# Two-layer feed-forward behind a delta-rule attention: weight splits by DMA, an early output factor, and the first substitution on another engine

## The chip, the cores and the metric

The kernel runs on one core of one Trainium2 chip. The time is the device time of one execution in microseconds; of several executions the median counts. An execution that was profiled leaves a trace: its span runs from the first to the last instruction. PE is the matrix engine, DVE, ACT and POOL are the vector, scalar and general engines, SP issues the transfers (DMA).

## The reference

A linear attention with the delta rule, then two feed-forward blocks on the heads put side by side (4 x 768 tokens, 8 heads of 48, so 384 features; hidden size 2048):

```python
k_n = k / (np.linalg.norm(k, axis=-1, keepdims=True) + 1e-06)
for t in range(S):
    y[:, :, t] = np.einsum('bhd,bhde->bhe', q[:, :, t], state)
    v_old = np.einsum('bhde,bhd->bhe', state, kt)
    state = state + bt[:, :, :, None] * np.einsum('bhd,bhe->bhde', kt, vt - v_old)
x = y.transpose(0, 2, 1, 3).reshape(B * S, H * D)
h = x @ w_in;  x = np.maximum(0.01 * h, h) @ w_out        # first block
h = x @ w2_in; x = (h - np.tanh(h)) @ w2_out              # second block
```

## The kernel before

**Data.** Every float32 operand of a matmul is split into two f16 parts, a high one and the rest (low), and a product is three matmuls: high x high, high x low, low x high. The four weight matrices arrive as 64-bit words; three integer instructions on DVE (`w_f32`: one tensor_scalar and two scalar_tensor_tensor) make float32 of them, in the place that the f16 parts will take. A weight is scaled by a power of two (`sw`), which needs its squared norm first. `Weights.splits` (L415) then goes over the 16 chunks of 384 columns of a matrix: ACT writes a scaled float32 copy `wst`, ACT makes the high half from it, and `tt` takes the difference on DVE or POOL. `wst` is a buffer of the ring "sx", of four buffers, which the layers' activations, `xhi`, `kn` and the output `osb` share.

**Work.** The 768 tokens are 12 stretches of 64 (n = 0 to 11), in 6 pairs u. For each pair the keys are normalized (`key_scale`, L547, a Newton iteration on DVE in small instructions), Gram matrices are made, and a triangular matrix of 32 x 32 for each of 32 blocks is inverted by forward substitution (`inverses`, L669): for column j a product and a sum, each over (31 - j) x j elements of a partition, 30 columns, 60 dependent instructions. Then come merges, states and outputs, which give x for n. The first block is layer (n, 0), the second layer (n, 1): eight steps `h_part` (18 matmuls of 256 columns), activation, split, and `o_part`. Order: (0,0), (1,0), (0,1), (1,1), then the next pair. `out_scale` (L1021) computes the factor of the output, three instructions on one column, at the end of a second layer, before ACT and DVE copy half of the output each from PSUM into `osb`.

**Order.** The program is written out by a planner that keeps a clock for each engine and a cost for each instruction. All side work (keys, inverses, weights "w", splits "s0" to "s3" and so on) consists of generators; each yields the time from which it wants to go on, and the one with the smallest time plus its bias (`d_i`, `d_w`, ...) goes next. The engines run their instructions in the order so written, and SP its transfers. The biases and some counts are read from START until all weights are converted ("w2"), from STEADY afterwards. `rows` is the number of columns of blocks solved on POOL; the rest is solved on DVE:

```python
for j in range(1, rows - 1):
    solve(pool, j, j + 1, rows)          # yields every third column
...
while rows < HB and jd < HB - 1:         # HB = 32
    for jd in range(jd, min(jd + 3, HB - 1)):
        solve(dve, jd, max(jd + 1, rows), HB)
    yield plan.t["dve"] - tune("look_inv")
```

With `rows` 32 all is on POOL. Since every instruction is issued through the planner, all have line 160 in the profile; they are told apart by engine and tile (X and Gd: the substitution; wi, wo: weights; wst: the scaled copy).

Of the kernel before, what the change touches and what calls it, by code (L numbers as in the profile page):

```python
# [7 lines left out]
F32 = mybir.dt.float32  # L8
F16 = mybir.dt.float16
BF16 = mybir.dt.bfloat16  # L10
I32 = mybir.dt.int32
ACTF = mybir.ActivationFunctionType
ALU = mybir.AluOpType
# [3 lines left out]

KS = 64.0
POW2 = 0x7F800000
START = {'cp': 1.0, 'lag': 4.0, 'look_pool': 3, 'look_inv': 0, 'lead_k': 1, 'lead_p': 7.5, 'd_v': 1, 'd_xa': 0, 'd_xb': 1, 'k_m': 2, 'd_s0': 1.0, 'd_s1': 1.0, 'd_s2': -1, 'd_s3': 0.5, 'bias_i': 3.5, 'bias': 1.5, 'rep': 4, 'every': 3, 'd_k0': 3, 'd_o': 0.5, 'd_s': 0.0, 'd_p': 0, 'd_m': 0, 'd_i': 0, 'd_g0': -2, 'd_q': 4.4, 'd_g': 0.5, 'd_k': 1, 'd_w': 0, 'rows': 32}  # L20
STEADY = {'cp': 5.5, 'lag': 4.0, 'look_pool': 3, 'look_inv': 2.5, 'lead_k': 1, 'lead_p': 7.5, 'd_v': 1, 'd_xa': -1, 'd_xb': 1, 'k_m': 2, 'd_s0': 1.0, 'd_s1': 1.0, 'd_s2': -1, 'd_s3': 0.5, 'bias_i': 3, 'bias': 1, 'rep': 6, 'every': 2, 'd_k0': 3, 'd_o': 0.5, 'd_s': 0.0, 'd_p': 0, 'd_m': 0, 'd_i': 0, 'd_g0': 0, 'd_q': 3.4, 'd_g': 0.0, 'd_k': 0, 'd_w': 0, 'rows': 32}


# [168 lines left out]
def kernel(  # L192
# [23 lines left out]
    DM = KT * 128  # L216
# [27 lines left out]
    def mm(o, lhsT, rhs, start=True, stop=True):  # L244
        pe.matmul(out=o, lhsT=lhsT, rhs=rhs, start=start, stop=stop)

    def copy(o, i, scale=1.0):
        act.activation(out=o, in_=i, func=ACTF.Copy, scale=scale)
# [4 lines left out]
    def tt(o, a, b, op, lead=2.0):  # L253

        f = {e: plan.finish(e, "tensor_tensor", [a, b], [o]) for e in ("dve", "pool")}
        (dve if f["dve"] + lead < f["pool"] else pool).tensor_tensor(out=o, in0=a, in1=b, op=op)
# [5 lines left out]
    def bias():  # L262
        return tune("bias_i" if "inverse" in done else "bias")
# [13 lines left out]
    def lo_of(o, i, scale, hi):  # L277
        dve.scalar_tensor_tensor(out=o, in0=i, scalar=scale, in1=hi, op0=ALU.mult, op1=ALU.subtract)
# [97 lines left out]
    class Weights:  # L376
# [36 lines left out]
            done.add((self.i, "s"))  # L413

        def splits(self):  # L415
            for f in range(NF):
                yield plan.t["act"]
                w = s_p.tile([128, DM], F32, tag="sx", name="wst")
                copy(w, self.f32[:, f], sw[:, self.i:self.i + 1])
                copy(self.dst[:, f, 0], w)  # L420
                tt(self.dst[:, f, 1], w, self.dst[:, f, 0], ALU.subtract, bias())
                done.add((self.i, f))

    def weights():
        wi = [words(w.rearrange("p f c n -> p (f c n)")) for w in WI2]
# [121 lines left out]
    def key_scale(a, y, t):  # L547

        dve.tensor_scalar(out=t, in0=a, scalar1=2.0 ** -100, scalar2=None, op0=ALU.max)
        dve.tensor_scalar(out=y.bitcast(I32), in0=t.bitcast(I32), scalar1=1, scalar2=POW2,  # L550
                          op0=ALU.logical_shift_right, op1=ALU.bitwise_and)
        dve.tensor_scalar(out=t, in0=y, scalar1=2.0 ** 64 / 0.85, scalar2=None, op0=ALU.mult)
        dve.reciprocal(out=y, in_=t)
        for it in range(5):
            if it in (1, 3):
                yield plan.t["dve"]
            dve.tensor_tensor(out=t, in0=y, in1=y, op=ALU.mult)
            dve.scalar_tensor_tensor(out=t, in0=t, scalar=-0.5, in1=a, op0=ALU.mult, op1=ALU.mult)
            dve.scalar_tensor_tensor(out=y, in0=t, scalar=1.5, in1=y, op0=ALU.add, op1=ALU.mult)
        dve.tensor_tensor(out=t, in0=a, in1=y, op=ALU.mult)  # L560
        dve.tensor_scalar(out=t, in0=t, scalar1=1e-6, scalar2=1.0 / KS, op0=ALU.add, op1=ALU.mult)
        dve.reciprocal(out=y, in_=t)
# [403 lines left out]
    def h_part(i, x, p, kap):  # L966

        ps = ps_h.tile([128, 2 * N], F32, tag="h", name="h_ps")
        order = [(t, a, b) for t in range(KT) for a, b in ((0, 0), (0, 1), (1, 0))]
        if p == 0:  # L970
            order = [(t, a, 0) for t in range(KT) for a in range(2)] + [(t, 0, 1) for t in range(KT)]
        for j in range(2):
            for n, (t, a, b) in enumerate(order):
                mm(ps[:, j * N:(j + 1) * N], WI[i][:, 2 * p + j, a, t], x[b][:, t], n == 0, n == 3 * KT - 1)
                if n % tune("every") == tune("every") - 1:
                    side.step()
        sx = s_p.tile([128, 2 * N], F32, tag="sx", name="sx")
        if i == 0:
            act.activation(out=sx, in_=ps, func=ACTF.Prelu, scale=C0, alpha=0.01)
        else:  # L980
            act.activation(out=sx, in_=ps, func=ACTF.Tanh, scale=kap[:, 0:1])
            dve.scalar_tensor_tensor(out=sx, in0=sx, scalar=kap[:, 1:2], in1=ps, op0=ALU.mult, op1=ALU.add)
        g = g_p.tile([128, 2, 2 * N], F16, tag="g", name="g")
        if i == 0:
            copy(g[:, 0], sx)
            tt(g[:, 1], sx, g[:, 0], ALU.subtract, bias())
        else:
            split(g[:, 0], g[:, 1], sx, C0)
        return g

    def o_part(i, po, g, p):

        for j in range(2):
            f = 2 * p + j
            first, last = f == 0, f == NF - 1
            gj = g[:, :, j * N:(j + 1) * N]
            for o in range(KT if i == 0 else 2):
                if i == 0 and o == 0 and first:
                    mm(po[0], maskp[:, 0:1].to_broadcast([128, 128]), maskp[:, 0:1].to_broadcast([128, 512]), True, False)
                for n, (a, b) in enumerate(((0, 0), (0, 1), (1, 0))):  # L1000
                    if i == 0:
                        mm(po[o // 2][:, o % 2 * N:o % 2 * N + N], WO[0][:, f, a, o * 128:(o + 1) * 128], gj[:, b],
                           o == 2 and first and n == 0, o > 0 and last and n == 2)
                    else:
                        mm(po[o][:, 0:DM], gj[:, b, o * 128:(o + 1) * 128], WO[1][:, f, a], first and n == 0,
                           last and n == 2)
                side.step()

# [12 lines left out]
    def out_scale(kap):  # L1021
        dve.tensor_scalar(out=kap[:, 2:3], in0=sw[:, 3:4], scalar1=C0, scalar2=None, op0=ALU.mult)
        dve.reciprocal(out=kap[:, 3:4], in_=kap[:, 2:3])
        dve.tensor_tensor(out=kap[:, 2:3], in0=kap[:, 3:4], in1=kap[:, 0:1], op=ALU.mult)
# [80 lines left out]
    def o_next():  # L1105
        n, i, p, g, kap, sx, po = pend.pop(0)
        if p == 0:
            po += [ps_o.tile([128, 512], F32, tag=f"o{o}", name=f"o{o}") for o in range(2)]
        need((2 * i + 1, 2 * p + 1))
        side.step(plan.at(g, WO[i][:, 2 * p], WO[i][:, 2 * p + 1]))  # L1110
        o_part(i, po, g, p)
        if p < NP - 1:
            return
        if i == 0:
            gen = to_xb(n, po, sx)
            e = side.add(gen, "xb")
            side.advance(e)
            return
        out_scale(kap)
        for o in range(2):  # L1120
            ob = s_p.tile([128, DM], F32, tag="sx", name="osb")
            if o % 2:
                dve.tensor_scalar(out=ob, in0=po[o][:, 0:DM], scalar1=kap[:, 2:3], scalar2=None, op0=ALU.mult)
            else:
                copy(ob, po[o][:, 0:DM], kap[:, 2:3])
            for h in range(2):
                r0 = (2 * o + h) * S + n * C
                sp.dma_start(out=out[r0:r0 + C], in_=ob[h * C:(h + 1) * C])

    def layer(n, i):  # L1130
        if i == 0:
            while ("n", n) not in done:
                if pend:
                    o_next()
                else:
                    side.force()
            x, sx = xa_t.pop(n)
            kap = None
        else:
            while ("m", n) not in done:  # L1140
                if pend:
                    o_next()
                else:
                    side.force()
            x, sx = xb_t.pop(n)
            need((2, "s"))
            kap = kappa(sx)
        po = []
        for p in range(NP):
            need((2 * i, 2 * p + 1))  # L1150
            side.step(max(at(x[0], WI[i][:, 2 * p]), ps_h.free("h")))
            g = h_part(i, x, p, kap)
            pend.append((n, i, p, g, kap, sx, po))
            if len(pend) > LAG:
                o_next()
        done.add(("ab"[i], n))
# [78 lines left out]
```

## Time and profile before

| | us |
|---|---|
| median of 3 runs | 1221.16 (1218.24 to 1222.01) |
| the profiled execution | 1222.18 |
| its span | 1220.3 |
| PE busy | 1013.1 (83%) |
| DVE busy | 736.5 (60%) |
| ACT busy | 634.0 (52%) |
| POOL busy | 509.1 (42%) |

The shares are means over a first part in which the weights are prepared and the first pair is computed, and a long second part with layers on the PE. The granted clock of the PE over the span was 0.97 of full speed.

### The profile page before, as it was taken

To read this page: it belongs to the slowest core of one execution; us is meant where nothing else is said; L and a number is where in the kernel's file an instruction comes from. 1 tells how busy PE (TensorE), PEld (TensorE's weight loads), DVE (VectorE), ACT (ScalarE), POOL (GpSimd) and SP (SyncE) were. 2 spreads that over 40 slices of the span, in tenths; PEclk is the share of its full clock that TensorE was granted. 3 is DMA by queue.
4 is the path that set the end of the run, shared out by engine and by line. 5 is a ranking of instruction groups with operands and counts; after the bars stand their busy time and mean duration, and the time that the engine had idled before them with its cause. 6 is when DMAs were issued, how large, how long until landed. Compare 5 with 4: busy or idle time off the path is not lost.

```text
span 1220.3 us, 36850 instructions
## 1 busy us (share of the span) xinstructions
PE 1013.1 (83%) x16216; PEld 831.8 (68%) x16216; DVE 736.5 (60%) x1592; ACT 634.0 (52%) x1409; POOL 509.1 (42%) x635
## 2 busy tenths in 40 slices
PE   0301658898798989989999888899999999999998
PEld 0201547686686878857787766678867888778875
DVE  7997896857567567777755665546753064420243
ACT  3555679695356655645567534435543364333332
POOL 4597446388214872483332682485110321012100
PEclk9999999899898989989999898999999999999999
DMA  9423133100001000000111000001000000000001
GB/s 363 154 84 113 55 106 96 37 24 1 16 23 39 24 22 17 26 23 24 39 32 37 24 1 16 10 8 33 25 10 14 14 12 2 11 17 1 1 1 27
DMA packets 21857, 48.17 MB, mean 39 GB/s; under 512 B 4288, under 2 KB 7360, under 8 KB 21696
## 3 DMA queue, kind: packets, MB, share of 16 engines
q1 hardware_dynamic: 21696, 45.82, 11.9%
q8 instruction: 126, 2.06, 0.7%
q14 instruction: 35, 0.29, 0.1%
HBM read 41.09 MB, written 4.72 MB: 38 GB/s over the span
## 4 chain that ended last, share of the span: by engine, by line
PE 51%; DVE 26%; ACT 11%; POOL 8%; issue 4%; DMA 0%; ACTq 0%; SPq 0%; DVEq 0%; POOLq 0%
PE o L160 21%; PE h_ps L160 19%; PE a_ps L160 11%; DVE n L160 4%; POOL X L160 3%; POOL Gd L160 3%; DVE x L160 2%; ACT g L160 2%; DVE wi L160 2%; DVE g L160 2%; DVE sx L160 2%; DVE wo L160 2%; ACT junk L160 1%; ACT sx L160 1%; DVE X L160 1%
## 5 line engine op out<-in xcount | busy, mean ns | idle before, releaser
L160 PE MATMUL h_ps<-x,wi 128*128 128x256 f16 x3456 | 427.9, 276 | 18.3 <-DVE x L160 12.3
L160 PEld LDWEIGHTS <-wi 128*128 128x128 f16 x3456 | 336.5, 99 | 77.6 <-issue 23.6
L160 PE MATMUL o<-wo,g 128*128 128x384 f16 x1152 | 214.9, 337 | 25.5 <-ACT osb L160 16.0
L160 POOL TENSOR_TENSOR g<-sx,g 128x512 f16<-128x512 f32 x78 | 93.1, 1194 | 311.6 <-ACT g L160 291.6
L160 PE MATMUL o<-g,wo 128*128 128x256 f16 x1728 | 210.6, 275 | 0.0
L160 PEld LDWEIGHTS <-wo 128*128 128x128 f16 x1728 | 167.4, 98 | 32.3 <-issue 10.5
L160 ACT ACTIVATE g<-sx 128x512 f16<-128x512 f32 x192 | 121.0, 630 | 120.2 <-DVE sx L160 117.2
L160 PEld LDWEIGHTS <-g 128*128 128x128 f16 x1152 | 113.7, 100 | 96.0 <-issue 36.0
L160 DVE SCALAR_TENSOR_TENSOR sx<-sx,kap,h_ps 128x512 f32<-128x512 f32 x96 | 71.2, 741 | 92.9 <-ACT sx L160 92.6
L160 POOL TENSOR_TENSOR Gd<-X 128x30 f32<-128x30 f32 (+9 forms) x180 | 110.8, 616 | 33.3 <-DVE X L160 19.5
L160 POOL TENSOR_TENSOR X<-X,Gd 128x30 f32<-128x30 f32 (+9 forms) x180 | 114.8, 638 | 14.1
L160 DVE SCALAR_TENSOR_TENSOR g<-sx,g 128x512 f16<-128x512 f32 x96 | 74.3, 774 | 67.4 <-ACT g L160 67.4
L160 ACT ACTIVATE sx<-h_ps,kap 128x512 f32<-128x512 f32 x96 | 65.4, 681 | 81.6 <-PE h_ps L160 71.3
L160 ACT ACTIVATE sx<-h_ps 128x512 f32<-128x512 f32 x96 | 56.5, 589 | 93.9 <-PE h_ps L160 87.6
L160 PEld LDWEIGHTS <-KTp 64*64 64x64 f16 x3360 | 66.2, 118 | 36.4 <-issue 34.4
L160 POOL TENSOR_TENSOR P<-P,maskp 128x1024 f16<-128x1024 f16 x24 | 52.6, 2196 | 61.4 <-DVE P L160 58.2
L160 PE MATMUL a_ps<-ab,ones 128*128 128x1 bf16 x124 | 11.7, 168 | 75.3 <-DVE ab L160 73.4
L160 PEld LDWEIGHTS <-KN 64*64 64x64 f16 x1824 | 37.5, 120 | 39.7 <-issue 35.7
L160 PE MATMUL a_ps<-Q,Sb 128*128 128x64 f16 x528 | 35.7, 199 | 13.2 <-DVE Sb L160 13.2
L160 PEld LDWEIGHTS <-ones 128*128 128x128 bf16 x124 | 7.8, 102 | 54.0 <-DVE ab L160 50.0
L160 PE MATMUL a_ps<-Q,KTp 64*64 64x64 f16 x1152 | 25.4, 201 | 23.1 <-ACT Q L160 20.2
L160 ACT ACTIVATE x<-a_ps,qs 32x128 f32<-32x128 f32 (+1 forms) x57 | 25.5, 447 | 31.4 <-PE a_ps L160 28.2
(161 smaller groups left out, 1533.1 us busy)
## 6 DMA issues: line engine op xcount, KB each, us to landing
wo<-in_w_in_dram SPq DMA_DIRECT2D x32, 384.0 KB, 6.1
qf<-in_q_dram SPq DMA_DIRECT2D x24, 256.0 KB, 2.6
wi<-in_w_out_dram SPq DMA_DIRECT2D x14, 384.0 KB, 7.8
kf<-in_k_dram SPq DMA_DIRECT2D x12, 384.0 KB, 4.1
vf<-in_v_dram SPq DMA_DIRECT2D x12, 384.0 KB, 4.1
out_dram<-osb SPq DMA_DIRECT2D x48, 96.0 KB, 2.2
wo<-in_w_out_dram SPq DMA_DIRECT2D x8, 384.0 KB, 3.8
stage<-in_w_out_dram SPq DMA_DIRECT2D x8, 384.0 KB, 3.8
```

The costliest lines, as they stand in the source:

```text
L160: return getattr(self.eng[eng], op)(*args, **kw)
```

## The change

- START gets `rows` 2: while the weights are not all converted, a substitution runs on DVE, in ten batches of three columns, and so do the three instructions behind it.
- `splits` goes over two chunks at once: ACT writes the scaled high half in f16 into a ring buffer, DVE makes the low half from the float32 source, the scale and that high half, into the first f16 place of the chunk, and a DMA on SP copies the high half into the second place. The matmuls read the two places in swapped order (`1 - a`).
- `key_scale` starts its Newton iteration from a better estimate and makes three rounds instead of five.
- `out_scale` moves from the end of a second layer to its start, behind `kappa`.

```diff
-START = {..., 'rows': 32}
+START = {..., 'rows': 2}
         def splits(self):
-            for f in range(NF):
+
+            s_ = sw[:, self.i:self.i + 1]
+            for f in range(0, NF, 2):
                 yield plan.t["act"]
-                w = s_p.tile([128, DM], F32, tag="sx", name="wst")
-                copy(w, self.f32[:, f], sw[:, self.i:self.i + 1])
-                copy(self.dst[:, f, 0], w)
-                tt(self.dst[:, f, 1], w, self.dst[:, f, 0], ALU.subtract, bias())
-                done.add((self.i, f))
+                w = s_p.tile([128, 2, DM], F16, tag="sx", name="wh")
+                copy(w, self.f32[:, f:f + 2], s_)
+                lo_of(self.dst[:, f:f + 2, 0], self.f32[:, f:f + 2], s_, w)
+                sp.dma_start(out=self.dst[:, f:f + 2, 1], in_=w)
+                done.update((self.i, f + i) for i in range(2))
     def key_scale(a, y, t):
         dve.tensor_scalar(out=t, in0=a, scalar1=2.0 ** -100, scalar2=None, op0=ALU.max)
-        dve.tensor_scalar(out=y.bitcast(I32), in0=t.bitcast(I32), scalar1=1, scalar2=POW2,
-                          op0=ALU.logical_shift_right, op1=ALU.bitwise_and)
-        dve.tensor_scalar(out=t, in0=y, scalar1=2.0 ** 64 / 0.85, scalar2=None, op0=ALU.mult)
-        dve.reciprocal(out=y, in_=t)
-        for it in range(5):
-            if it in (1, 3):
+        dve.tensor_scalar(out=t.bitcast(I32), in0=t.bitcast(I32), scalar1=1, scalar2=None,
+                          op0=ALU.logical_shift_right)
+        dve.tensor_scalar(out=y.bitcast(I32), in0=t.bitcast(I32), scalar1=-1.0, scalar2=float(0x5F375A00),
+                          op0=ALU.mult, op1=ALU.add)
+        for it in range(3):
+            if it == 1:
                 yield plan.t["dve"]
...
-                mm(ps[:, j * N:(j + 1) * N], WI[i][:, 2 * p + j, a, t], x[b][:, t], n == 0, n == 3 * KT - 1)
+                mm(ps[:, j * N:(j + 1) * N], WI[i][:, 2 * p + j, 1 - a, t], x[b][:, t], n == 0, n == 3 * KT - 1)
...
-        out_scale(kap)
         for o in range(2):
             ob = s_p.tile([128, DM], F32, tag="sx", name="osb")
...
             kap = kappa(sx)
+            out_scale(kap)
```

`o_part` gets the same `1 - a` in both of its matmuls.

## Rows read from the trace of the kernel before

**Rows 1.** Windows by stage: length, busy us (instructions) of PE, PEld, DVE, ACT, POOL.

```profile
48.00:107.20 59.20, 2.84 (x83) 2.58 (x84) 52.97 (x79) 30.23 (x74) 52.87 (x66) 1.00 0.35 118
107.20:181.70 74.50, 35.97 (x1138) 34.05 (x1138) 65.69 (x111) 52.56 (x120) 36.87 (x33) 1.00 0.31 101
181.70:381.40 199.70, 177.63 (x2910) 144.28 (x2910) 132.99 (x302) 130.91 (x320) 96.99 (x120) 0.94 0.12 34
381.40:820.00 438.60, 397.51 (x7144) 325.20 (x7145) 284.20 (x646) 233.82 (x574) 233.02 (x317) 0.95 0.08 22
```

**Rows 2.** The chain of waits, 0 to 320 us, its shares by line.

```profile
by line: POOL X L160 12.6%; POOL Gd L160 10.4%; DVE wi L160 8.5%; issue 7.2%; DVE wo L160 6.1%; DVE n L160 6.0%; DVE x L160 3.5%; PE a_ps L160 3.4%; DVE X L160 2.5%; ACT g L160 2.2%; DVE g L160 1.7%; ACT wo L160 1.6%; POOL wi L160 1.6%; ACT
```

**Rows 3.** POOL's timeline: start, duration, instruction [idle before]; substitution's first, product with beta.

```profile
50.00 0.85 POOL L160 TENSOR_TENSOR Gd<-X 128x30 f32<-128x30 f32 x1 [2.81 <-DVE X L160]
...
107.26 2.34 POOL L160 TENSOR_TENSOR X<-X,bt 128x1024 f32<-128x1024 f32 x1
```

**Rows 4.** PE's timeline: first matmuls of layers (0, 0) and (2, 0).

```profile
181.70 5.79 PE L160 MATMUL h_ps<-x,wi 128*128 128x256 f16 x27 [5.57 <-DVE x L160]
...
381.45 0.93 PE L160 MATMUL h_ps<-x,wi 128*128 128x256 f16 x5 [1.28 <-DVE x L160]
```

**Rows 5.** DVE's timeline, 17 to 27 us: single durations.

```profile
17.76 0.95 DVE L160 SCALAR_TENSOR_TENSOR wi<-wo,wi 128x768 int32<-128x768 int32 x1
...
24.58 0.18 DVE L160 TENSOR_TENSOR x<-x 128x32 f32<-128x32 f32 x1
24.80 0.42 DVE L160 SCALAR_TENSOR_TENSOR x<-x 128x32 f32<-128x32 f32 x2
...
26.75 0.56 DVE L160 TENSOR_TENSOR kn<-kf,x 128x384 f32<-128x384 f32 x1
```

**Rows 6.** Groups by form on DVE, 50 to 107.2 us: busy us, mean ns.

```profile
L160 DVE SCALAR_TENSOR_TENSOR wo<-wi,wo 128x768 int32<-128x768 int32 x14 | 17.6, 1254 | 0.4
L160 DVE TENSOR_TENSOR wi<-wst,wi 128x384 f16<-128x384 f32 x8 | 8.0, 1002 | 2.1 <-ACT wi L160 2.1
L160 DVE SCALAR_TENSOR_TENSOR wi<-wo,wi 128x768 int32<-128x768 int32 x7 | 7.4, 1063 | 0.2
L160 DVE TENSOR_SCALAR wo<-wi 128x768 int32<-128x768 int32 x7 | 6.1, 872 | 0.0
L160 DVE SCALAR_TENSOR_TENSOR wo<-x,wo 128x384 int32<-128x384 int32 x4 | 4.2, 1063 | 0.0
```

**Rows 7.** Windows of the splits (tile wst): length, DVE, ACT, POOL; sum from 48 us.

```profile
107.20:181.70 74.50, 0.54 (x1) 26.23 (x48) 27.13 (x25) 1.00 0.31 101
...
sum 252.00, DVE 13.69 ACT 70.98 POOL 51.13; mean DVE 4.56 ACT 23.66 POOL 17.04
```

**Rows 8.** Groups by form, 0 to 320 us: the split of x on ACT and DVE.

```profile
L160 ACT ACTIVATE xhi<-x,sxs 128x768 f16<-128x768 f32 x4 | 3.7, 924 | 0.2 <-DVE n L160 0.2
...
L160 DVE SCALAR_TENSOR_TENSOR x<-x,sxs,xhi 128x768 f16<-128x768 f32 x4 | 4.1, 1020 | 5.1 <-ACT xhi L160 5.1
```

**Rows 9.** Timelines: the last weight scale, a split between pair 1's solve steps.

```profile
229.28 0.16 DVE L160 RECIPROCAL sw<-p 128x1 f32<-128x1 f32 x1
...
264.39 0.91 POOL L160 TENSOR_TENSOR wo<-wst,wo 128x384 f16<-128x384 f32 x1
```

**Rows 10.** DMA issues, 100 to 300 us: count, KB each, median us to landing.

```profile
qf<-in_q_dram SPq DMA_DIRECT2D x5, 256.0 KB, 2.6
```

**Rows 11.** Timelines at the end of layer (0, 1).

```profile
325.41 0.58 ACT L160 ACTIVATE osb<-o,kap 128x384 f32<-128x384 f32 x1 [1.28 <-DVE kap L160]
325.43 0.62 DVE L160 TENSOR_SCALAR osb<-o,kap 128x384 f32<-128x384 f32 x1
...
326.05 0.65 PE L160 MATMUL o<-wo,g 128*128 128x384 f16 x3 [4.15 <-ACT osb L160]
```

**Rows 12.** Tile osb, whole span: its own waits, then who waited for it.

```profile
  DVE kap L160: 13.0, 7
...
  PE o L160: 19.6, 8
```

More of the change, by code (lines that the diff above doesn't have):

```diff
@@ L19 @@
 POW2 = 0x7F800000
-START = {'cp': 1.0, 'lag': 4.0, 'look_pool': 3, 'look_inv': 0, 'lead_k': 1, 'lead_p': 7.5, 'd_v': 1, 'd_xa': 0, 'd_xb': 1, 'k_m': 2, 'd_s0': 1.0, 'd_s1': 1.0, 'd_s2': -1, 'd_s3': 0.5, 'bias_i': 3.5, 'bias': 1.5, 'rep': 4, 'every': 3, 'd_k0': 3, 'd_o': 0.5, 'd_s': 0.0, 'd_p': 0, 'd_m': 0, 'd_i': 0, 'd_g0': -2, 'd_q': 4.4, 'd_g': 0.5, 'd_k': 1, 'd_w': 0, 'rows': 32}
+START = {'cp': 1.0, 'lag': 4.0, 'look_pool': 3, 'look_inv': 0, 'lead_k': 1, 'lead_p': 7.5, 'd_v': 1, 'd_xa': 0, 'd_xb': 1, 'k_m': 2, 'd_s0': 1.0, 'd_s1': 1.0, 'd_s2': -1, 'd_s3': 0.5, 'bias_i': 3.5, 'bias': 1.5, 'rep': 4, 'every': 3, 'd_k0': 3, 'd_o': 0.5, 'd_s': 0.0, 'd_p': 0, 'd_m': 0, 'd_i': 0, 'd_g0': -2, 'd_q': 4.4, 'd_g': 0.5, 'd_k': 1, 'd_w': 0, 'rows': 2}
 STEADY = {'cp': 5.5, 'lag': 4.0, 'look_pool': 3, 'look_inv': 2.5, 'lead_k': 1, 'lead_p': 7.5, 'd_v': 1, 'd_xa': -1, 'd_xb': 1, 'k_m': 2, 'd_s0': 1.0, 'd_s1': 1.0, 'd_s2': -1, 'd_s3': 0.5, 'bias_i': 3, 'bias': 1, 'rep': 6, 'every': 2, 'd_k0': 3, 'd_o': 0.5, 'd_s': 0.0, 'd_p': 0, 'd_m': 0, 'd_i': 0, 'd_g0': 0, 'd_q': 3.4, 'd_g': 0.0, 'd_k': 0, 'd_w': 0, 'rows': 32}
@@ L1001, in o_part @@
                     if i == 0:
-                        mm(po[o // 2][:, o % 2 * N:o % 2 * N + N], WO[0][:, f, a, o * 128:(o + 1) * 128], gj[:, b],
+                        mm(po[o // 2][:, o % 2 * N:o % 2 * N + N], WO[0][:, f, 1 - a, o * 128:(o + 1) * 128], gj[:, b],
                            o == 2 and first and n == 0, o > 0 and last and n == 2)
                     else:
-                        mm(po[o][:, 0:DM], gj[:, b, o * 128:(o + 1) * 128], WO[1][:, f, a], first and n == 0,
+                        mm(po[o][:, 0:DM], gj[:, b, o * 128:(o + 1) * 128], WO[1][:, f, 1 - a], first and n == 0,
                            last and n == 2)
```

## The prediction

> **What bounds the kernel now.** I read the windows by stage first. In 48 to 107 us the PE is busy 2.8 of 59.2 us while DVE (53.0) and POOL (52.9) are full; in 107 to 181.7 the PE has half of the stretch and DVE 65.7 of 74.5; in 181.7 to 381.4 the PE is busy 178 of 200, then 398 of 439 [rows 1]. So the first 181.7 us are a prologue in which the PE starves, and behind it the PE is the bound with 22 and 41 us of idle time in those two. The chain of waits over the first 320 us says what the prologue is made of: POOL X and Gd (the forward substitution) on top, 23%, then DVE's weight words [rows 2]. On POOL's timeline the substitution of pair 0 runs from 50.0 to the product with beta, which ends at 107.26 + 2.34 = 109.6 [rows 3]. The first matmul of layer (0, 0) waits for x at 181.70, and that of pair 1 at 381.45, again for x with 1.28 us of idle PE [rows 4]: after each start a pair has 200 us of PE work, so an earlier first start is kept only if pair 1's x comes earlier too.
>
> **The substitution on DVE.** POOL loses 60 instructions, DVE gains 60 on the same shapes: twice the sum of j(31 - j), 9,920 elements per partition. DVE's price early in the run: 0.18 us for 32 elements, a dependent one starts 0.22 us after it, and 0.56 us for 384 elements, so 1.08 ns an element [rows 5]. That is 60 x 0.22 + (9,920 - 1,920) x 1.08 ns = 13.2 + 8.6 = 21.8 us. The upper bound is what company costs: the weights' tensor_tensor of 384 took 1.00 instead of 0.56 while POOL was busy [rows 5, 6], so 39 us. I take 21.8, since the work that kept POOL busy in this stretch is just what leaves it.
>
> Here one rule of the Trainium skill bears (SBUF — State Buffer, Who interferes with whom): a DVE instruction with two SBUF inputs and a POOL instruction that reads SBUF exclude each other, and the later one blocks. The rows agree that such DVE instructions stretch beside POOL [rows 5, 6]. By the rule the solve would take the low end as long as POOL is empty, and the same sum comes out.
>
> The DVE is shared, so what lies between the solve's ten batches decides. In 48 to 107 us the weight words took 25 scalar_tensor_tensor (17.6 + 7.4 + 4.2 us) and, by the code, 13 tensor_scalar (7 of them 6.1 us, so about 10.4), the splits 8.0 us; the rest of 53.0 is 5.4 [rows 1, 6]. A solve batch and the weights both ask again at the time DVE comes free, with the same bias 0, so I expect them to alternate: 11 weight instructions at 0.95 [rows 5], 10.5 us. W1_in's 8 new splits add 8.2 (price below). The end: 50.0 + 21.8 + 10.5 + 8.2 + 5.4 + 1.3 for the product with beta = 97.2 instead of 109.6, 12.4 us earlier. With none of the weights between it is 86.7 (22.9 earlier), with all 38 it is 122.8 (13.2 later); the break-even is 24.
>
> **The splits.** Before, 64 chunks cost ACT two activations each, 71 us, and their subtraction went to POOL (51.1) and DVE (13.7) [rows 7]. After, 32 double chunks cost one activation of 768 elements, 0.92 us, and one scalar_tensor_tensor of 768 into f16, 1.02 us, the form of x's own split [rows 8]. ACT: 71 - 29.6 = 41 us less; POOL: 51 less; DVE: 32.6 - 13.7 = 19 more. From 107 to 181.7 the chain to layer (0, 0) meets 8.2 us of them on DVE instead of 0.5; against that stand the stretching that POOL's 27.1 us of splits leave off [rows 7] (at 5.0 us for 52.9 us of POOL, from the 21 long instructions' 1.25 and 1.06 over 0.95 [rows 1, 5, 6], some 2.6), 1.3 us of key_scale, and about 4 us from ACT, a third of the 12 it gets back there (26.2 us of 52.6 becomes some 15). I put this at zero, bounds -8 and +4. Layer (0, 0) starts 12 us earlier, near 169.
>
> What is late next: the 27 weight instructions that no longer run under POOL's solve, 22 to 26 us of DVE, fall behind 97 us. "w1" is done some 20 us later, and with it pair 1's keys start later. DVE has room for it (133 of 200 us busy in 181.7 to 381.4 [rows 1]), but not for free. For pair 1 speak six single splits of 0.91 us that stood between the steps of its own solve on POOL and are gone, 5.5 us [rows 9], and ACT's 41 us, since its key norms are small ACT work. I keep 8 of the 12 us (bounds 0 and 12, or 23 if nothing interleaves) at the start of pair 1. Only pair 0 changes engine: the last weight scale is there at 229 us and pair 1's solve runs around the split at 264, so STEADY holds for it [rows 9].
>
> **The copy of the high halves by DMA.** 32 more transfers of 192 KB on SP, each behind its DVE instruction. The nearest row is q's 256 KB, 2.6 us to landing [rows 10]. It holds one of four "sx" buffers for those 2.6 us and holds back what stands behind it on SP: weight loads, q, k. I cost it at nothing, since weights are split well ahead of their layer; the bound is 32 x 2.6 = 83 us if every one were waited for, and a few us (of the last split chunks, between the first tanh layers) is what I allow.
>
> **key_scale.** Seven fewer instructions, of them two rounds of 0.18 + 0.42: about 1.3 us at the start, and as much for each later step, hidden later under PE.
>
> **The output's factor.** Three small instructions leave the end of each second layer. There the ACT copy of the output waits for them behind DVE's queue: at 325.41 after 1.28 us, and the PE's next o waits 4.15 us for that copy [rows 11]. Over the run ACT waits 13.0 us at 7 of 12 such places and PE 19.6 us at 8 [rows 12]. DVE's own half of the output, 0.62 us, still stands in the same queue and comes only the three instructions earlier, 0.65 us, and PE can do its first half meanwhile. So per place between 0.65 and 1.3: for the four places of pairs 0 to 3 with long waits 2.6 to 5.2, for the others 1.0 to 1.3 in all; sum 3.6 to 6.5, I take 4. Put behind kappa they cost 0.65 us at each layer's start, under its first matmuls.
>
> **The swapped halves** in the matmuls change addresses only.
>
> **Sum.** The profiled run took 1222.2 us (span 1220.3 and 1.9 around it), 1.0 above the median. 1222.2 - 8 - 4 = 1210.2, so 1209 in the median.
>
> **Rivals.** *Pair 1 holds it back* (0.22): its keys are so late that x comes at 381 us all the same, the 12 us become idle PE at the border of the layers, and the output's factor alone counts: 1222.2 - 4 - 1.0 = 1217. For it: the wait at 381.45 is for x already. Against: the 5.5 us and ACT's relief. *More than planned* (0.10): the solve runs with hardly a weight between, and the backlog is absorbed: 22.9 + 6.5 off, 1192. For it: DVE idle 67 us after 181.7. Against: equal biases. *DVE becomes the bound* (0.16), the other sign: the plan keeps all 38 weight instructions between the batches, the solve ends 13 us late, and layer (0, 0) with it: 1222.2 + 13 - 4 - 1 = 1230. It decides from 24 such instructions on; DVE was 89% busy there without the solve [rows 1]. *It does not do what it says* is not one of them: START holds at 50 us in any case, the weights being ready much later.
>
> **How the numbers follow.** The forecast has 0.52, its own range 1201 to 1217 (kept 0 to 12, factor 3.6 to 6.5, some 4 us either way since the planner redraws all that follows). No change is within 0.3%, 1217.5 to 1224.8, about what this kernel's measurement can tell. Faster: nearly all of the forecast, half of pair 1's case, the larger gain: 0.73; same: the other half and the edges: 0.13; slower: 0.14. The range 1195 to 1224 leaves out most of the 0.16 and half of the 0.10.
>
> **What would show it.** Right: the last solve step on DVE near 95 us with about ten weight instructions between; layer (0, 0) near 169; wst gone from ACT and POOL; the ACT copy of the output no longer waiting for kap; x of pair 1 near 373. Wrong: the solve beyond 110 us; PE idle before pair 1's first matmul; ACT waiting for an "sx" buffer, that is for a DMA of high halves; w2_out's splits not done when the output of the first tanh layer needs them.

## The result and the profile after

The kernel after takes 1203.91 us in the median (1200.98 to 1206.82, 4 runs) against 1221.59 (1218.24 to 1222.67) of the kernel before in the same session: ratio 0.9858, 95% interval 0.9843 to 0.9874, so 17.3 us less. The forecast was 1209, in a range of 1195 to 1224. The profiled execution took 1202.04 us, with a span of 1200.2. Below, a difference between two kernels is the difference of their ratios to before, times 1221 us; the intervals make such a difference sure to some 3 us.

The windows of after, cut as in [rows 1] (the same columns; behind them the granted clock as a share of full speed):

```profile
48.00:107.20 59.20, 5.54 (x170) 4.95 (x172) 53.99 (x127) 20.04 (x36) 3.77 (x3) 0.50 0.40 136
107.20:181.70 74.50, 56.85 (x1215) 50.38 (x1212) 63.04 (x126) 47.77 (x109) 11.41 (x11) 0.69 0.31 97
181.70:381.40 199.70, 159.44 (x2914) 127.70 (x2912) 153.04 (x302) 119.25 (x305) 87.30 (x108) 0.92 0.20 63
381.40:820.00 438.60, 400.57 (x7413) 332.00 (x7412) 274.12 (x608) 234.63 (x563) 240.34 (x329) 0.96 0.08 23
```

POOL's 52.9 us of the first stretch have gone to 3.8. PE has 56.9 us of work in the second stretch instead of 36.0, but in the third it has 18 us less: it idles 40 us there, not 22, of them 18 between 192 and 222 us. From PE's timeline (as in [rows 4]: the first matmuls of layers (0, 0), (1, 0) and (2, 0); in brackets the idle time ahead of each and what ended it):

```profile
148.07 0.80 PE L160 MATMUL h_ps<-x,wi 128*128 128x256 f16 x3 [7.09 <-DVE x L160]
...
222.02 3.74 PE L160 MATMUL h_ps<-x,wi 128*128 128x256 f16 x18 [2.06 <-DVE x L160]
...
371.30 1.74 PE L160 MATMUL h_ps<-x,wi 128*128 128x256 f16 x11 [2.77 <-DVE x L160]
```

Layer (0, 0) starts 33.6 us earlier than in [rows 4], and pair 1 at 371.30, 10.2 earlier. The gain is neither kept from there on nor made there: (2, 1) starts 17 us later than before, (4, 0) 8 us later, (6, 0) 12 earlier, (8, 0) 18.7 earlier, and from there nothing changes. So the starts alone don't say which part did what; the experiments do.

The splits and weights on DVE, 48 to 107.2 us, against [rows 6] (busy us, mean ns), and the view of the new ring tile wh over the whole span:

```profile
L160 DVE SCALAR_TENSOR_TENSOR wo<-wi,wo 128x768 int32<-128x768 int32 x10 | 9.5, 952 | 0.1
L160 DVE SCALAR_TENSOR_TENSOR wi<-wi,sw,wh 128x768 f16<-128x768 f32 x8 | 8.0, 1015 | 1.5 <-ACT wh L160 1.5
...
L160 DVE TENSOR_SCALAR wo<-wi 128x768 int32<-128x768 int32 x6 | 3.3, 557 | 0.0
```

```profile
L160 ACT ACTIVATE wh<-wi,sw x16: 917/919/936, 56.9 to 218.5; 128x768 f16<-128x768 f32 x16
...
who waited for it (us, times):
  DVE wo L160: 5.0, 5
  DVE wi L160: 2.4, 6
  ACT junk L160: 1.3, 1
...
DMA to landing us min/median/max: 2.3/2.3/4.2
```

With POOL empty the weight instructions take 952 and 557 ns instead of 1254 and 872, and the copies of the high halves land after 2.3 us with one engine waiting 1.3 us. In the view of osb, against [rows 12], DVE's kap is gone from what osb's engines wait for, and "PE o" from those that wait for osb.

### The profile page after: what moved, and what is told of

Its sections match the earlier page's. It is cut to its first block, busy times and chain, and to the rows that moved or that the text cites. A ratio compares the mean times of both kernels' runs of the same rounds, so it can differ in the third digit from the quotient of the medians.

```text
span 1200.2 us, 36728 instructions
## 1 busy us (share of the span) xinstructions
PE 1002.9 (84%) x16216; PEld 825.5 (69%) x16216; DVE 735.4 (61%) x1593; ACT 596.6 (50%) x1313; POOL 420.3 (35%) x525
## 4 chain that ended last, share of the span: by engine, by line
PE 49%; DVE 25%; ACT 10%; POOL 8%; issue 5%; DMA 3%; SPq 0%; ACTq 0%; POOLq 0%; DVEq 0%
PE o L160 19%; PE h_ps L160 18%; PE a_ps L160 12%; POOL X L160 4%; POOL Gd L160 3%; DVE wi L160 3%; DVE x L160 2%; DVE wo L160 2%; ACT junk L160 2%; DVE X L160 2%; DVE n L160 2%; DVE g L160 2%; ACT g L160 2%; DMA wo<-in_w_in_dram 1%; DVE sx L160 1%
## 5 line engine op out<-in xcount | busy, mean ns | idle before, releaser
L160 PE MATMUL o<-wo,g 128*128 128x384 f16 x1152 | 205.8, 328 | 3.3 <-ACT x L160 3.3
L160 POOL TENSOR_TENSOR g<-sx,g 128x512 f16<-128x512 f32 x72 | 86.0, 1196 | 342.3 <-ACT g L160 336.7
L160 PEld LDWEIGHTS <-KTp 64*64 64x64 f16 x3360 | 63.1, 115 | 58.1 <-issue 55.0
L160 POOL TENSOR_TENSOR Gd<-X 128x30 f32<-128x30 f32 (+9 forms) x150 | 89.9, 599 | 29.9 <-DVE X L160 18.7
L160 POOL TENSOR_TENSOR X<-X,Gd 128x30 f32<-128x30 f32 (+9 forms) x150 | 93.8, 625 | 11.7
L160 POOL TENSOR_TENSOR P<-P,maskp 128x1024 f16<-128x1024 f16 x24 | 55.5, 2314 | 103.8 <-DVE P L160 91.2
L160 DVE TENSOR_TENSOR g<-sx,g 128x512 f16<-128x512 f32 x24 | 26.8, 1118 | 39.7 <-ACT g L160 37.5
L160 PEld LDWEIGHTS <-Sb 128*128 128x128 f16 x528 | 30.2, 103 | 23.2 <-DVE Sb L160 22.5
L160 DVE COPY Ub<-R 64x768 f16<-64x768 f16 x44 | 23.3, 531 | 33.5 <-PE a_ps L160 32.7
```

The costliest lines, as they stand in the source:

```text
L160: return getattr(self.eng[eng], op)(*args, **kw)
```

## Experiments

**One part alone.** First each part of the change was put alone into the kernel before, and the planner wrote the program anew.

The factor (`out_scale(kap)` behind `kappa`), nothing else. 

> The kernel before, and of the change only the output's factor moved to the layer's start. As predicted from the waits alone it gains 4 us (3.6 to 6.5). By the trace before and after it should be more, 8 to 12 us: the PE's idle time before the next o ran to 5 us at three places, and the matmuls behind it then ran at half the granted clock (12 matmuls in 4.00 us instead of 2.11). The rival, a lucky new order of the whole program, expects any value within some 10 us of the kernel before, either way, and ACT's waits for the factor gone all the same.

Measured: 1219.37 us, ratio 0.9978 (0.9961 to 0.9996): 2.7 us less, under both expected sizes.

The solve on DVE (`'rows': 2` in START), nothing else. 

> The kernel before, and of the change only the substitution of pair 0 on DVE. Theory: the solve ends near 95 to 100 us, layer (0, 0) starts 20 to 30 us earlier (the weights, and with them pair 1's keys, fall behind and leave pair 0's chain), and the total gains 4 to 10 us. The rival that the splits' relief of ACT and POOL makes the prologue's gain expects layer (0, 0) less than 10 us earlier and no gain in the total.

Measured: 1244.24 us, ratio 1.0183 (1.0156 to 1.0210); layer (0, 0) starts at 162.2, (2, 0) at 401.2.

The splits with the swapped halves, nothing else. 

> The kernel before, and of the change only the splits (high half by DMA, two chunks at once, swapped places). Theory: POOL's solve of pair 0 loses its four split instructions, some 5 us, layer (0, 0) starts 5 to 10 us earlier, the total gains 2 to 8 us. The rival that the splits make the whole prologue's gain expects layer (0, 0) 20 us or more earlier.

Measured: 1233.43 us, ratio 1.0090 (1.0060 to 1.0120); layer (0, 0) at 165.6, (2, 0) at 385.7.

The three rounds of `key_scale`, nothing else. 

> The kernel before, and of the change only the three Newton rounds with the better start. Theory: 1 to 2 us less at the start, all else hidden: no change that can be told, 1217 to 1222. If the new order of the program alone moves the time by 5 us or more either way, it shows here, since the part itself is small.

Measured: 1238.24 us, ratio 1.0125 (1.0092 to 1.0157).

Three of the four parts make the kernel slower when they stand alone, the keys by 15 us although they only take work away. Either the parts need each other, or these runs measure something else: the planner writes another program for each. The next runs keep the program's order.

**One part undone, in the order of after.** The planner books the costs and dependences of the new form, and the instructions of the old form are issued in its place; `g_` engines book without issuing, `r_` engines issue without booking. PE, ACT, POOL and SP then have the same instructions in the same order as in after, except for the part itself.

```diff
+        out_scale(kap, r_dve)
         for o in range(2):
...
             kap = kappa(sx)
-            out_scale(kap)
+            out_scale(kap, g_dve)
```

> Every instruction stands in the order of the kernel after on every engine; only the three VectorE instructions of the output's factor are issued late again, behind the last o. Theory 1 (the parts act where they stand, as the prediction has it): the eight waits of TensorE for the output come back, some 2 to 2.5 us each in seven of them, and TensorE falls to half its clock behind some, as before did behind three of them (1.9, 1.9 and 1.4 us); 4 to 10 us in all, so 1208 to 1214 us. Theory 2 (the gain is the planner's new order and the parts themselves are worth little): within 0.3% of after, 1200 to 1208 us.

Measured: 1213.39 us, ratio 0.9923 (0.9902 to 0.9944), 7.9 us over after.

The place is the end of layer (0, 1). After, from ACT's, DVE's and PE's timelines:

```profile
315.80 1.69 PE L160 MATMUL a_ps<-X,AT 64*64 64x32 f16 x96 [1.55 <-DVE X L160]
...
316.92 0.56 ACT L160 ACTIVATE osb<-o,kap 128x384 f32<-128x384 f32 x1
...
317.53 0.69 ACT L160 ACTIVATE PM<-a_ps,half 128x512 f16<-128x512 f32 x1
```

With the late factor:

```profile
315.33 2.74 PE L160 MATMUL a_ps<-X,AT 64*64 64x32 f16 x96 [1.13 <-DVE X L160]
...
317.18 1.91 DVE L160 STREAM_TRANSPOSE XF<-Gd 128x1024 f32<-128x1024 f32 x1
...
318.96 0.14 DVE L1026 TENSOR_SCALAR kap<-sw 128x1 f32<-128x1 f32 x1
...
319.61 0.58 ACT L160 ACTIVATE osb<-o,kap 128x384 f32<-128x384 f32 x1 [3.06 <-DVE kap L1028]
...
320.08 0.68 ACT L160 ACTIVATE PM<-a_ps,half 128x512 f16<-128x512 f32 x1
```

The factor stands behind a transpose of 1.91 us, ACT idles 3.06 us for it, and `PM<-a_ps`, which stands behind osb on ACT, comes 2.55 us later though it has nothing to do with the output (0.58 us of that is not the factor's: the 96 matmuls a_ps that it reads end at 318.07 instead of 317.49). The windows that follow, first of after, then with the late factor:

```profile
325.00:330.00 5.00, 4.04 (x208) 3.51 (x201) 3.22 (x6) 2.47 (x5) 1.72 (x3) 1.00 0.01 3
330.00:335.00 5.00, 4.42 (x131) 3.59 (x126) 3.09 (x8) 2.69 (x8) 1.87 (x4) 1.00 0.01 3
335.00:340.00 5.00, 5.00 (x130) 3.93 (x128) 4.06 (x13) 1.32 (x2) 0.00 (x0) 1.00 0.01 3
```

```profile
325.00:330.00 5.00, 3.57 (x165) 3.40 (x165) 2.90 (x5) 2.79 (x9) 0.68 (x2) 0.69 0.01 3
330.00:335.00 5.00, 5.00 (x117) 3.61 (x115) 1.72 (x4) 2.38 (x8) 2.92 (x5) 0.50 0.03 7
335.00:340.00 5.00, 5.00 (x106) 3.94 (x103) 2.69 (x8) 0.98 (x2) 0.00 (x0) 0.50 0.02 3
```

In these 15 us PE does 388 matmuls where after does 469, and those of 256 columns take 417 ns in the mean instead of 274 (first after, then the late factor, 325 to 340 us):

```profile
L160 PE MATMUL h_ps<-x,wi 128*128 128x256 f16 x29 | 4.0, 274 | 0.0
```

```profile
L160 PE MATMUL h_ps<-x,wi 128*128 128x256 f16 x16 | 4.0, 417 | 0.0
```

Wait and slow clock together put pair 1's first matmul at 377.16 instead of 371.30, 5.9 us behind the first two second layers. Over the run osb waited this long (in the first fence after, in the second the late factor):

```profile
  PE o L160: 32.4, 7
who waited for it (us, times):
```

```profile
  PE o L160: 31.0, 6
  DVE kap L1028: 18.8, 8
who waited for it (us, times):
  PE o L160: 4.8, 5
```

PE hardly waits for osb itself (4.8 us), so the expected waits did not come back. The page's first line with the late factor (after's is shown with the keys below) says where the time went:

```profile
PE 1013.6 (83%) x16216; PEld 833.6 (69%) x16216; DVE 736.9 (61%) x1593; ACT 597.4 (49%) x1313; POOL 420.2 (35%) x525
```

With the same 16216 matmuls PE is busy 10.7 us longer than in after and idle 3.2 us longer (spans 1214.1 and 1200.2). At the place shown, the delay comes through what ACT's queue holds behind osb, and slower matmuls follow; that it is so at every other place is not shown.

**The solve.**

```diff
-                solve(dve, jd, max(jd + 1, rows), HB)
+                solve(g_dve, jd, max(jd + 1, rows), HB)
+                solve(r_pool, jd, max(jd + 1, rows), HB)
```

Only the 60 steps go back to POOL; the product with beta stays on DVE.

> The order of the kernel after, with the first pairs' forward substitution (30 instructions) on GpSimd. Theory 1: layer (0,0) starts some 11 us later (the solve took 33.4 us in before's trace, 109.6 to the product against 98.6 in after), at about 159 us; if the start of pair 1's layers still hangs on pair 0, all of it is lost, 1213 to 1216 us, and if 8 of 12 are kept as the prediction has it, 1210 to 1213. Theory 2: TensorE waits from 192 to 222 us in after for the second pair anyway, so the start is hidden behind that; layer (1,0) starts within 2 us of 222 and the time is within 0.3% of after.

Measured: 1200.88 us, ratio 0.9835 (0.9815 to 0.9855); 2.8 us under after, the two intervals overlap. In the views of tile X, first after, then this kernel (L689 and L691 are the two instructions of a step on POOL; times ns min/median/max, then first and last start in us):

```profile
L160 DVE TENSOR_TENSOR X<-X,Gd x30: 191/350/409, 49.2 to 96.6; 128x30 f32<-128x30 f32 x2, 128x58 f32<-128x58 f32 x2, 128x84 f32<-128x84 f32 x2, 128x108 f32<-128x108 f32 x2
...
L160 DVE TENSOR_TENSOR X<-X,bt x1: 1226/1226/1226, 97.4 to 97.4; 128x1024 f32<-128x1024 f32 x1
```

```profile
L691 POOL TENSOR_TENSOR X<-X,Gd x30: 248/628/1315, 50.0 to 96.5; 128x30 f32<-128x30 f32 x2, 128x58 f32<-128x58 f32 x2, 128x84 f32<-128x84 f32 x2, 128x108 f32<-128x108 f32 x2
...
L160 DVE TENSOR_TENSOR X<-X,bt x1: 1226/1226/1226, 96.8 to 96.8; 128x1024 f32<-128x1024 f32 x1
```

POOL is as early with the solve as DVE, 96.8 against 97.4 us, though its single steps are slower, since DVE does weights in between. Before, POOL came to the product at 107.26 [rows 3]: four subtractions of weights stood in its queue there (5.3 us in all, in the view by groups of that stretch), and its 60 steps took 47.53 us instead of 43.08. So half of the 10.5 us comes from the splits that left POOL. The shorter steps do not: in the kernel with three parts in before's order, further down, the splits have left POOL too, the steps take 47.7 us and POOL comes to the product at 101.64. They belong to the order of after; which instructions beside them make the difference was not taken apart.

**The keys.** `key_scale` books three rounds and issues the five, with the start and the reciprocal of before: one round at the first of its two places, four at the second.

```diff
-    def key_scale(a, y, t):
+    def planned(a, y, t, dve):
...
+        steps = iter([lambda: (start_old(), rounds(1)), lambda: (rounds(4), end())])
+        for at_ in planned(a, y, t, g_dve):
+            next(steps)()
+            yield at_
+        next(steps)()
```

> The order of the kernel after, with the scale of the keys made in five rounds and a reciprocal again, 9 more VectorE instructions of 16 elements (about 0.13 us each, 1.2 to 1.3 us a time). Theory 1: hidden from pair 1 on, 1 to 2 us in the prologue; 1202 to 1208 us. Theory 2 (the order): the same, within 0.3% of after. So the two agree here; it is the run of the part alone (which was 17 us slower than before) that this one holds against: 15 us or more over after would say that the three rounds themselves are what after lives from.

Measured: 1214.78 us, ratio 0.9947 (0.9928 to 0.9966), 10.9 us over after, a miss for both theories. The first lines of the page, after and this kernel:

```profile
PE 1002.9 (84%) x16216; PEld 825.5 (69%) x16216; DVE 735.4 (61%) x1593; ACT 596.6 (50%) x1313; POOL 420.3 (35%) x525
```

```profile
PE 1006.3 (83%) x16216; PEld 825.8 (68%) x16216; DVE 754.7 (62%) x1670; ACT 596.9 (49%) x1313; POOL 418.7 (35%) x525
```

77 instructions more (seven a time, not the nine expected) cost DVE 19.3 us, 0.25 us each, not the 0.13 that both theories counted with; and over half of it, 10.9 us, comes out at the end. PE's idle time, span less busy time, grows from 197.3 to 206.8 us.

**The splits.** The old two activations and a subtraction on POOL for each chunk (all 64 on POOL, where before had 49 of them), no DMA.

```diff
-                copy(w, self.f32[:, f:f + 2], s_)
-                lo_of(self.dst[:, f:f + 2, 0], self.f32[:, f:f + 2], s_, w)
-                sp.dma_start(out=self.dst[:, f:f + 2, 1], in_=w)
+                g_act.activation(out=w, in_=self.f32[:, f:f + 2], func=ACTF.Copy, scale=s_)
+                g_dve.scalar_tensor_tensor(out=self.dst[:, f:f + 2, 0], in0=self.f32[:, f:f + 2], scalar=s_, in1=w,
+                                           op0=ALU.mult, op1=ALU.subtract)
+                g_sp.dma_start(out=self.dst[:, f:f + 2, 1], in_=w)
+                for i in range(2):
...
+                    r_act.activation(out=wst, in_=self.f32[:, f + i], func=ACTF.Copy, scale=s_)
+                    r_act.activation(out=self.dst[:, f + i, 1], in_=wst, func=ACTF.Copy, scale=1.0)
+                    r_pool.tensor_tensor(out=self.dst[:, f + i, 0], in0=wst, in1=self.dst[:, f + i, 1], op=ALU.subtract)
```

> The order of the kernel after, with the weights split through a scaled float32 copy (two ScalarE instructions and one GpSimd subtraction a chunk; no DMA). Theory 1: 36 more ScalarE instructions of 0.6 to 0.9 us and 36 GpSimd subtractions in the prologue that hold up VectorE's two-operand work; layer (0,0) starts 8 to 17 us later and the time is 1209 to 1220 us. Theory 2 (the order): starts move, but the end stays within 0.3% of after.

Measured: 1225.92 us, ratio 1.0044 (1.0025 to 1.0062), 22.7 us over after. Layer (0, 0) starts only 4.5 us later, (1, 0) 16, pair 1 29.4. Groups on POOL, 107 to 300 us (busy us, mean ns, idle ahead of the group and what ended it):

```profile
L160 POOL TENSOR_TENSOR g<-sx,g 128x512 f16<-128x512 f32 x13 | 15.7, 1208 | 22.3 <-ACT g L160 21.4 <-DVE n L160 0.9
...
L432 POOL TENSOR_TENSOR wo<-wh,wo 128x384 f16<-128x384 f32 x13 | 12.8, 984 | 34.8 <-ACT wo L431 34.8
...
L432 POOL TENSOR_TENSOR wi<-wh,wi 128x384 f16<-128x384 f32 x8 | 7.6, 951 | 18.2 <-ACT wi L431 18.1
```

POOL waits 53 us for ACT's copies, and the first layers' own subtractions `g<-sx,g` stand in the same queue. ACT has 96 activations more, 39 us (596.6 to 635.9). Which of the two makes the 22.7 us was not taken apart.

**Parts in the order of before.** The same method the other way round.

`key_scale` books five rounds and issues three. 

> Every instruction in the order of the kernel before, with the scale of the keys made by three rounds from a first guess instead of five (7 VectorE instructions of 16 elements fewer, ten times). Theory 1 (the parts act where they stand; the slower time of this part alone, 1238 us, was the planner's other order): 12 us of VectorE work fewer from pair 1 on, of which most shows, as the 11 us did that five rounds cost in the order of after; 1208 to 1215 us. Theory 2 (three rounds do harm here by themselves): 1230 us or more. If VectorE's small work is hidden in this order, as my prediction had it: within 0.3% of before, 1217 to 1225.

Measured: 1214.27 us, ratio 0.9928 (0.9910 to 0.9946): 8.8 us under before. The same part alone in a program written anew was 15 us over before. So those 24 us are the price of the planner's other order, and a run of one part alone says little about the part.

`out_scale` is booked late and issued early. 

> Every instruction in the order of the kernel before; only the three VectorE instructions of the output's factor are issued early, at the head of their layer. It is the term of 4 us (3.6 to 6.5) that my prediction took for this part, measured in the order for which it was worked out. The prediction's term: 1214 to 1218 us. Theory 1 with the size that the order of after showed (9.5 us, VectorE's two transposes stand ahead of the late factor there): 1211 to 1214 us. Rival (in this order the output's two copies stand behind other work of ScalarE and VectorE anyway; with the factor early, TensorE still waited 12.6 us in all for them in the run with three parts, of 19.6): within 0.3% of before, 1218 to 1225 us.

Measured: 1217.19 us, ratio 0.9947 (0.9926 to 0.9968): 6.5 us under before. PE still waits 12.4 us at 6 places for osb, of the 19.6 in [rows 12].

Splits, keys and factor of after together; the solve stays on POOL. A pair of chunks is issued at the place of its second chunk. 

> Every instruction in the order of the kernel before, with three of the four parts of the change (splits without the scaled float32 copy, three rounds, the output's factor early); the first solve stays on GpSimd and in its old order. Theory 1: the parts act where they stand and nearly add up; in the order of after the three undone cost 9.5, 10.9 and 22 us one at a time, of which the cover of the others takes some; 1190 to 1209 us, so as fast as after or faster, with no new order needed. Theory 2 (the gain needs the order that the planner draws for the new parts): 1214 us or more.

Measured: 1206.73 us, ratio 0.9869 (0.9844 to 0.9894): 16.0 us under before, no measurable difference to after. Keys and factor alone sum to 15.3, so, if parts add up, the splits add 0.7 us in this order, with some 5 us of doubt either way; no run put the splits alone into it. Layer (0, 0) starts at 183.5 us there, even later than before, and the end is as early as after's.

**Fewer small instructions on DVE, in the order of after.** Since the keys showed such work to count, more of it was cut: powers of two inverted by integer arithmetic on their exponents, and the constant products of the factors made once.

```diff
-        dve.tensor_scalar(out=t[:, 0:1], in0=t[:, 1:2], scalar1=2.0 ** 64 / top, scalar2=None, op0=ALU.mult)
-        dve.reciprocal(out=o, in_=t[:, 0:1])
+        g_dve.tensor_scalar(out=t[:, 0:1], in0=t[:, 1:2], scalar1=2.0 ** 64 / top, scalar2=None, op0=ALU.mult)
+        g_dve.reciprocal(out=o, in_=t[:, 0:1])
...
+        r_dve.tensor_scalar(out=o.bitcast(I32), in0=t.bitcast(I32)[:, 1:2], scalar1=-1.0, scalar2=k, op0=ALU.mult,
+                            op1=ALU.add)
...
+        r_dve.scalar_tensor_tensor(out=kap[:, 1:2], in0=sx[:, 0:1], scalar=kc[0][:, 0:1], in1=sx[:, 1:2],
+                                   op0=ALU.mult, op1=ALU.mult)
...
+        r_dve.tensor_tensor(out=kap[:, 2:3], in0=kc[0][:, 1:2], in1=kap[:, 0:1], op=ALU.mult)
```

The last two stand for four instructions of `kappa` and the three of `out_scale`.

> Every instruction in the order of the kernel after, with the small VectorE work (one element a partition) cut further: the powers of two that scale each tile made by three instructions instead of four (64 times), the factors of the second pair of layers by three instead of six and of the output by one instead of three (12 times); some 120 instructions of 0.15 to 0.16 us fewer, 19 us, about 15 of them ahead of 850 us. Theory 1 (VectorE's queue, in order, stands on the chain of the first six pairs, so that its small work counts nearly one for one, as it did with the keys): 8 to 15 us under after, 1189 to 1196 us. Theory 2 (such work is hidden beside TensorE, and only the keys' scale was exposed): within 0.3% of after, 1200 to 1207 us.

Measured: 1193.25 us (1192.53 to 1193.89), ratio 0.9761 (0.9744 to 0.9777): 11.8 us under after, the fastest kernel of this study. Its page's first line:

```profile
PE 1001.6 (84%) x16216; PEld 824.4 (69%) x16216; DVE 717.0 (60%) x1473; ACT 597.8 (50%) x1313; POOL 419.8 (35%) x525
```

120 instructions and 18.4 us of DVE are gone. Three measurements with the order held still agree on what such a microsecond is worth: 8.8 of 15.2 (DVE 736.5 to 721.3, keys in before's order), 10.9 of 19.3, 11.8 of 18.4, so 0.56 to 0.64, each sure to some 0.2.

The first matmul of some layers, in us, from PE's timelines. These are the profiled executions; they lie up to 6 us from the medians (1231.88 us with the old splits, where the median is 1225.92), so the table shows where time is gained or lost, and the medians how much:

```
kernel             (0,0)   (1,0)   (2,0)   (4,0)   (6,0)   (8,0)    span
before             181.7   235.0   381.4   567.1   770.1   943.0  1220.3
fix_keys_new       179.0   232.5   377.9   561.8   759.1   931.8  1208.7
fix_factor_early   181.7   234.7   380.2   565.4   769.0   939.9  1215.8
fix_three_new      183.5   233.0   374.9   557.8   757.7   928.3  1204.2
after              148.1   222.0   371.3   575.3   758.0   924.3  1200.2
fix_solve_pool     147.5   221.0   371.0   571.8   756.1   922.7  1198.6
fix_factor_late    148.1   221.6   377.2   580.1   771.9   937.4  1214.1
fix_keys_old       149.8   224.9   377.4   583.1   770.8   937.2  1213.1
fix_splits_old     152.6   238.0   400.7   603.0   787.5   954.3  1230.2
few_small          147.1   220.3   370.8   569.0   751.0   915.8  1191.6
```

## Why the prediction was right, and which steps were not

**The time** lies within the range, on the side of the forecast; the sum was 12 us and the gain 17.3. But the sum gave 8 of its 12 to the prologue and 4 to the factor, and that is not how the gain is made up: in the order of before the keys give 8.8, the factor 6.5 and the splits nothing that could be told; the solve was not run in that order, and in after's it gives nothing. The prologue's 8 us stand in the sum for what the keys gave, so that the time came out is in good part luck.

**"The substitution on DVE"** had its end right, 97.4 + 1.2 = 98.6 us for 97.2, partly by luck: 20 weight instructions stood between the batches, not 11, but at 14.2 us for 10.5, and the solve began 1.0 us earlier. The comparison was wrong. The step held DVE among weights against POOL as it was before; in the order of after, with the splits gone from it, POOL finishes the same solve at the same time, and the kernel is no slower with it. So this edit is worth nothing there.

**Layer (0, 0) near 169, pair 1 near 373.** They came at 148.1 and 371.3. The first is not due to any one part: undone in after's order each leaves it between 147.5 and 152.6, and with three parts in before's order it is at 183.5. It belongs to the order that the planner drew, and 20.6 of the 33.6 us are lost again before (1, 0), for PE idles between the two. That the kept start equals the forecast 8 us so nearly is chance, since the layers fall back behind before by (2, 1).

**key_scale "hidden later under PE"** is the step that failed. The count of instructions was right, seven a time, but PE hides little of it: three rounds give 8.8 us in before's order, and five cost 10.9 in after's, though DVE is only 61% busy over the span. Whether the small instructions cost by holding up what stands behind them in DVE's queue, or as links of the chain to the next pair's x themselves, these runs don't tell apart. The size was short too, 15 to 19 us of DVE instead of 14. DVE's timeline of after shows why:

```profile
439.06 0.18 DVE L160 TENSOR_TENSOR n<-n 128x16 f32<-128x16 f32 x1
439.15 2.29 POOL L160 TENSOR_TENSOR g<-sx,g 128x512 f16<-128x512 f32 x2 [3.38 <-ACT g L160]
439.27 2.20 DVE L160 SCALAR_TENSOR_TENSOR n<-n 128x16 f32<-128x16 f32 x2
441.51 0.17 DVE L160 TENSOR_TENSOR n<-n 128x16 f32<-128x16 f32 x1
```

Two instructions on 16 elements, 0.17 us each when alone, take 2.20 us, because each lasts as long as the POOL instruction beside it. The Trainium skill has the rule (SBUF — State Buffer, Who interferes with whom): a DVE instruction with two SBUF inputs and a GpSimd instruction that reads SBUF exclude each other, and the later one is blocked for the whole of the other. The trace agrees: of after's 150 instructions on 16 elements of the keys (tile n) 26 are longer than 0.27 us, 17.9 us together, and each of these ends 28 to 34 ns after a POOL instruction, while the other 124 take 0.18 us in the mean. Eight of the 26 are of the kind TENSOR_SCALAR, with a single tensor input, of which the rule as told here does not speak. The prediction used it for the solve alone.

**The factor, 4 us (3.6 to 6.5)**, gave 6.5 in the order for which it was worked out, the upper bound, and there its mechanism holds: PE's waits for osb fell by 7.2 us (19.6 to 12.4). In the order of after it is worth 7.9 by another way, which the sum had not: PE waits only 4.8 us for osb, and the delay comes through the work behind osb on ACT and slower matmuls afterwards.

**The DMA of the high halves at nothing** was right: 2.3 us to landing and 1.3 us of waiting for a buffer. **The splits at zero** (bounds -8 and +4) hold in before's order as far as it can be told (0.7 us, some 5 of doubt); in the order of after they are worth 22.7, since that order is written around an empty POOL. Undone one at a time there, the parts sum to 38.7 us, over twice the gain: an order made for the new parts is a bad one for the old.

**The planner's redraw** was put at "some 4 us either way". It is the largest number here: 24 us for the keys alone (1.0125 against 0.9928), 4 us for the factor alone (0.9978 against 0.9947). For the whole change it comes to nothing measurable, 0.9858 against 0.9869 in the old order (there without the solve on DVE). A forecast that rests on one redrawn program has this uncertainty whatever its terms are.

**The rivals.** "Pair 1 holds it back" would have shown 381 us and 1217. "More than planned" put 1192; layer (0, 0) started even earlier than it supposed, but that start was not kept. "DVE becomes the bound" put the solve's end at 122.8 us, and it came at 98.6; what DVE's small work costs shows with the later pairs. What stays open is why the planner's orders for single parts are so much worse; no run here took such an order apart.

## What to carry to other kernels

Where a scheduler writes the program, measure a part with the order held still (book one form, issue the other); a part alone in a program written anew measures the order. A busy share of 61% does not say that an engine's small work is hidden: here a microsecond of small instructions on it was worth 0.56 to 0.64 at the end, in three measurements. When an edit moves work off an engine, ask first what the edits beside it already take off that engine.

## What was not expected of the hardware

In after, PE's granted clock was recorded as 0.50 (1.2 of 2.4 GHz) from 48 to 148 us, in the kernel with the solve on POOL as 1.00. Over 107.2 to 128 us the same kind of work, small matmuls, took the same time in both (first after):

```profile
107.20:128.00 20.80, 17.58 (x585) 16.95 (x582) 14.98 (x30) 7.81 (x14) 2.54 (x3) 0.50 0.01 3
```

```profile
107.20:128.00 20.80, 17.59 (x571) 16.87 (x568) 14.95 (x31) 7.81 (x14) 1.94 (x3) 1.00 0.01 4
```

That is not because such matmuls don't feel the clock. The product a_ps<-X,AT, from PE's timelines, first of after, then of the kernel with the solve on POOL, then of after again, later:

```profile
105.75 5.30 PE L160 MATMUL a_ps<-X,AT 64*64 64x32 f16 x192 [2.01 <-DVE X L160]
```

```profile
105.15 5.30 PE L160 MATMUL a_ps<-X,AT 64*64 64x32 f16 x192 [2.00 <-DVE X L160]
```

```profile
322.11 1.69 PE L160 MATMUL a_ps<-X,AT 64*64 64x32 f16 x96
```

At 105 us one of them takes 27.6 ns in either kernel; at 322 us, at 0.91 to 1.00, 17.6; with the late factor at 315 us, at 0.50, 28.5 (96 in 2.74 us). So both kernels ran these matmuls at the pace of the half clock, and the 1.00 recorded for one of them does not show in their durations. The kernel before recorded 1.00 there as well [rows 1] and took 5.30 us for the same 192, at 120.83 us. The half clock recorded in after's prologue is therefore no cost that the kernel before did not have. Why the records differ stays open.
